# Attention's value products in three runs per pair of heads instead of four

## The chip, the cores and the metric

The kernel runs on one core of one Trainium2 chip. The metric is the device time of one execution in microseconds. Five engines work side by side, each through its own instructions in the order in which the program lists them: TensorE (PE, with its weight loads PEld), VectorE (DVE), ScalarE (ACT), GpSimd (POOL) and SyncE (SP), which issues the transfers. They meet at semaphores.

## The reference

```
q, k, v: (4 batches, 8 heads, 576 positions, 64)   all float32
scores = q k^T / 8 + bias(head, i, j)        # bias: a small two-layer net of log distances
attn   = softmax(scores)                     # row maximum taken off, divided by the row sum
x      = attn v                              # -> 2304 tokens x 512
x      = (h - tanh(h)) w_out,   h = x w_in                     # first layer, 512 -> 2048 -> 512
out    = (s relu(h)^2 + b) w2_out, h = x w2_in                 # second layer
```

## The kernel before, in words

**Stages.** The bias of every head is made first and goes to DRAM. Attention follows, then the two layers. All is float32, and the layers split each operand into a rounded upper part and a rest.

**Attention.** Work goes pair by pair: two heads of one batch, 16 pairs. A pair has five *periods*, one for each tile `t` of query rows: `t` = 0 to 3 are 128 rows of each head, `t` = 4 holds the last 64 rows of both heads in one tile. There are 80 periods, and the loop `for n in range(NK + 6)` takes each through a pipeline over the following turns. In turn `n` the program lists, in this order:

- `emit_norm(n - 2)`, POOL: the exponentials times the inverse row sum, into tile `pn`;
- `emit_score(n)`, PE: the scores into two PSUM tiles `s` (one for each head; there are two buffers);
- `emit_exp(n - 1)`, ACT: the exponentials with their row sums;
- `emit_bias(n)`, DVE: bias added to the scores, row minimum taken (`raw`, `mn`); this frees the tile `s`;
- `emit_transpose(n - 3)`, PE: `pn` is transposed 64 rows at a time into two PSUM banks `t0` and `t1` (and `c` for the tail columns of `t` = 0 and 1);
- `emit_parts(n - 3)`, the "bank copies": ACT copies `t0`, DVE copies `t1` into the tile `pt` of the unit. For `t` = 4 each makes three small copies. The banks have one buffer, so the next turn's transposes wait for both;
- `emit_sum(n - 1)` and `emit_inverse(n - 1)`, DVE: the inverse of the row sums;
- the value products of this turn (`emit_pv`, PE) from the table `PV`, and `emit_out` behind the last of a unit: ACT copies the result `o` to `xo`, SP stores it;
- the transfers of `FT` and `work`, then the weight steps of `TK`, then `PRE` (the first products of the first layer).

A pair has two *units* of value products: unit 0 (rows 0 to 255, `t` = 0 and 1) and unit 1 (rows 256 to 575). A unit is five key blocks `j`; each `j` is two products side by side, one for each head. The table gives unit 0 three blocks in turn 5i+6 and two in 5i+7, and unit 1 three in 5i+8 and two in 5i+10: four runs per pair, all at the end of their turn. As L436, L480 and L539 the profile shows scores, transposes and value products; their forms name the part of the array that they use (64\*128 for scores and transposes, 64\*64 for the scores of `t` = 4, 128\*64 for value products).

**Weight steps.** Eleven weight tiles of the layers are loaded during attention, and the first eight of them go through four steps there. `fetch(k)` loads tile `k` (turn 1 for `k` = 0). Step 0, `begin`, is one POOL and one ACT instruction on the loaded tile (L142, L143); steps 1 and 2, `high` and `low`, are one DVE instruction each (L148, L153); step 3, `both`, is a cast on ACT, a subtraction on POOL (L159, L98) and a store. `TK` says in which turn each is listed.

**After attention.** The first layer's first 512 tokens run in a plain loop; the rest of both layers goes in five groups `q`, each of eight steps `p`. In the groups 0 and 1 the function `keeps` lists the preparation of the second layer's weights at named places: `"S"` (start), `"A"` (middle) and `"E"` (end) of step `p`, and `"T"` (the tail of a group): load (`keep_raw`), `keep_begin`, `keep_value` (two DVE instructions and a store).

Of the kernel before, what the change touches and what calls it, by code (L numbers as in the profile page):

```python
# [19 lines left out]
B, H, S, D = 4, 8, 576, 64  # L20
# [27 lines left out]
FT = {1: 0, **{4 + 4 * k: k for k in range(1, 11)}}  # L48
ND = 8
TK = {}  # L50
for j, n in enumerate(sorted([41, *range(8, 80, 5)])):
    for m, step in ((n - n % 5, 0), (n, 1)) if j % 2 == 0 else ((n, 2), (n + 3, 3)):
        TK.setdefault(m, []).append((j // 2, step))
TK.update({82: [(8, 0)], 83: [(9, 0), (8, 1), (8, 2)], 84: [(10, 0), (9, 1), (9, 2)], 85: [(10, 1), (10, 2)]})
PR = [(0, 2), (2, 3)]
XPRE = [(-22, "load", 0), (-20, "hi", 0), (-19, "lo", 0), (-18, "load", 1), (-16, "hi", 1), (-15, "lo", 1),
        (-12, "load", 2), (-9, "hi", 2), (-8, "lo", 2), (-5, "load", 3), (-2, "hi", 3), (-1, "lo", 3)]


CHUNKS = [(0, 0, 512)]  # L60
# [6 lines left out]
def tile_kernel(ctx, tc, qk, vd, wcat, wts, sb, ltab, ipsi8, out):  # L67
# [39 lines left out]
    raw_w = {}  # L107
# [29 lines left out]
    def begin(k, raw):  # L137

        hw = raw[:, :, 1].bitcast(F32)
        x, sg = place(f"s{(0, 1, 6)[k % 3] if k < 32 else (0, 1, 6, 4, 5)[k % 5]}", [512]), place(f"s{2 + k % 2}", [512])  # L140
        y = ypool[0].tile([128, 512], F32, tag="y", name="y") if ypool else x
        nc.gpsimd.tensor_scalar(out=sg, in0=hw, scalar1=0.0, scalar2=1.0, op0=ALU.mult, op1=ALU.mult)  # L142
        nc.scalar.activation(out=y, in_=hw, func=AF.Copy, scale=2.0 ** -112)  # L143
        wx_t[k] = (raw, x, y, sg)
# [86 lines left out]
    with ExitStack() as c0:  # L231
# [63 lines left out]
        for n in range(NG + 2):  # L295
            if n < NG:
# [3 lines left out]
                for g in range(4 * G, 4 * G + 4):  # L300
                    hid = hids[g] = hp_.tile([128, LW], F32, tag="h", name="hid")
                    k = min(range(2), key=lambda k: held[k] + HC[k][0] + HC[k][1] * nd)
# [88 lines left out]
    with ExitStack() as ca:  # L391
# [15 lines left out]
        load, hi, lo = load_x(0)  # L407
# [30 lines left out]
        def emit_bias(x):  # L438
            i, t = periods[x]
            for j, k, _ in heads_of(x):  # L440
                raw = sp.tile([128, S], F32, tag="raw", name="raw", bufs=3)
                mn = sp.tile([128, 1], F32, tag="mn", name="mn", bufs=3)
                nc.vector.tensor_tensor_reduce(  # L443
                    out=raw.rearrange("p (c j) -> p c j", c=2), in0=s_t.pop((x, j))[:, :, 0:288],
                    in1=bias_t[pairs[i][0], k].rearrange("p (c j) -> p c j", c=2),
                    scale=-0.125, scalar=3.0e38, op0=ALU.add, op1=ALU.min, accum_out=mn)
                raw_t[x, j] = (raw, mn)

                if i >= 2 and bq and 36 - len(bq) < 11 + i // B * 9 + (max(0, k + 1) if i % B == B - 1 else 0):
                    load_bias(*bq.pop(0))  # L450

        def emit_exp(x):
            sm = sums[x] = sp.tile([128, 2], F32, tag="sm", name="sm", bufs=4)
            for j, _, _ in heads_of(x):
                raw, mn = raw_t.pop((x, j))
                p = p_t[x, j] = pp.tile([128, S], F32, tag="p", name="p")
                nc.scalar.activation(out=p, in_=raw, func=AF.Exp, scale=-1.0, bias=mn, accum_out=sm[:, j:j + 1])  # L457
# [72 lines left out]
        def emit_pv(i, u, j):  # L530

            r0, n = UNITS[u]
            v = v_t[i]
            if j == 0:
                o_t[i, u] = ps_o.tile([128, 512], F32, tag="o", name="o")[:, 0:n]
            o = o_t[i, u]
            for e in range(2):
                h = slice(e * 64, e * 64 + 64)
                nc.tensor.matmul(o[h], v[:, e, j], unit_t[i, u][:, 8 if j == 4 else 4 * e + j, 0:n], start=(j == 0), stop=(j == 4))  # L539

        def emit_out(i, u):
            hp, b = pairs[i]
            r0, n = UNITS[u]
            del unit_t[i, u]
            xo = sp.tile([128, 320], F32, tag="xo", name="xo", bufs=2)[:, 0:n]
            nc.scalar.copy(xo, o_t.pop((i, u)))
            nc.sync.dma_start(out=x1_d[hp][:, b * S + r0:b * S + r0 + n], in_=xo)
# [3 lines left out]

        PV = {}
        for i in range(len(pairs)):
            for u, (m, parts) in enumerate(((5 * i + 6, (3, 2)), (5 * i + 8, (3, 0, 2)))):
                js = list(range(5))
                for c, k in enumerate(parts):
                    PV.setdefault(m + c, []).append((i, u, js[:k]))
                    js = js[k:]
        for n in range(NK + 6):
            def now(lag):  # L560
                return 0 <= n - lag < NK

            if n == NK:
                s_ctx.close()
                for pool, name in ((hpool, "ps_h"), (ypool, "ps_y")):
                    pool.append(h_ctx.enter_context(tc.tile_pool(name=name, bufs=2, space=PSUM, side="right", reuse_waits="tile")))
            if now(2):
                emit_norm(n - 2)
            if now(0):
                emit_score(n)  # L570
            if now(1):
                emit_exp(n - 1)
            if now(0):
                emit_bias(n)
            if now(3):
                emit_transpose(n - 3)
                emit_parts(n - 3)
            if now(1):
                emit_sum(n - 1)
                emit_inverse(n - 1)  # L580
            for i, u, js in PV.pop(n, []):
                for j in js:
                    emit_pv(i, u, j)
                if 4 in js:
                    emit_out(i, u)
            if n in FT:
                fetch(FT[n])
            for f in work.pop(n, []):
                f()
            for k, j in TK.get(n, []):  # L590
                if j:
                    (high, low, both)[j - 1](k)
                else:
                    begin(k, raw_w.pop(k))
            for f in PRE.get(n, []):
                f()
        assert not PV
        assert not work
    qk_ctx.close()
# [2 lines left out]
    with ExitStack() as cb:  # L602
# [58 lines left out]
        def plan(at, g, j):  # L661
            KEEPS.setdefault(at, []).append((g, j))

        j = 0
        for P in range(1, 16):
            q, p = divmod(P, 8)
            three = P in (9, 11)
            for jj, at in ((j, "A"), (j + 1, "E")):
                plan((q, p, at), keep_value, jj)
                if P != 8:  # L670
                    plan((q, p - 1, "A" if P in (10, 12) else "S"), keep_raw, jj)
                    plan((q, p - 1, "E"), keep_begin, jj)
                else:
                    plan((0, 12, "T"), keep_raw, jj)
                    plan((0, 15, "T"), keep_begin, jj)
            if three:
                plan((q, p, "S"), keep_raw, j + 2)
                plan((q, p, "A"), keep_begin, j + 2)
                plan((q, p, "E"), keep_value, j + 2)
            j += 2 + three  # L680
# [3 lines left out]
        for n, f in enumerate(turns):  # L684
            if f not in ring_f.values():
# [5 lines left out]
                x = 16 - NR + n if n < 3 else max(ring_f, key=next_use)  # L691
# [188 lines left out]
        for _ in range(3):  # L880
            n, f, x, _ = back.pop(0)
# [209 lines left out]
```

## Time and profile before

| | |
|---|---|
| time, median of 3 runs | 1030.69 us (1029.17 to 1031.68) |
| the profiled execution's own time | 1030.39 us |
| its span, first to last instruction | 1028.6 us |
| PE busy | 1016.7 us (99%) |
| DVE, ACT, POOL busy | 719.7, 591.5, 571.5 us |
| attention's scores, first to last turn | 47.7 to 256.6 us |
| granted TensorE clock, in every slice | full speed |

The span is cut into times from its start. "Idle before" is the time that an engine stood still just before an instruction, and the name behind `<-` is what ended that. Matmuls are pipelined and their ends are modelled, so "busy" PE says only that no gap is seen; distances between starts say more.

### The profile page before, as it was taken

To read this page: it belongs to the slowest core of one execution; us is meant where nothing else is said; L and a number is where in the kernel's file an instruction comes from. 1 tells how busy PE (TensorE), PEld (TensorE's weight loads), DVE (VectorE), ACT (ScalarE), POOL (GpSimd) and SP (SyncE) were. 2 spreads that over 40 slices of the span, in tenths; PEclk is the share of its full clock that TensorE was granted. 3 is DMA by queue.
4 is the path that set the end of the run, shared out by engine and by line. 5 is a ranking of instruction groups with operands and counts; after the bars stand their busy time and mean duration, and the time that the engine had idled before them with its cause. 6 is when DMAs were issued, how large, how long until landed. Compare 5 with 4: busy or idle time off the path is not lost.

```text
span 1028.6 us, 18742 instructions
## 1 busy us (share of the span) xinstructions
PE 1016.7 (99%) x6664; PEld 830.9 (81%) x6664; DVE 719.7 (70%) x1478; ACT 591.5 (58%) x1241; POOL 571.5 (56%) x706
## 2 busy tenths in 40 slices
PE   9999999999999999999999999999999999999998
PEld 4366666666687799999788888999889998899986
DVE  8888888888478788876877776455675556655541
ACT  8888888888466555544544444455545444454441
POOL 3276676687468678840767431598516663076400
PEclk9999999999999999999999999999999999999999
DMA  8857575743399658867577648411202112031000
GB/s 293 316 190 252 182 254 170 229 152 103 113 360 340 250 206 280 285 210 250 196 268 235 205 143 291 154 41 42 100 14 93 45 58 92 3 104 49 1 32 31
DMA packets 68205, 170.48 MB, mean 166 GB/s; under 512 B 7312, under 2 KB 13584, under 8 KB 68112
## 3 DMA queue, kind: packets, MB, share of 16 engines
q1 hardware_dynamic: 67536, 168.80, 47.9%
q8 instruction: 52, 0.85, 0.3%
q10 hardware_dynamic: 576, 0.48, 0.1%
q14 instruction: 41, 0.34, 0.1%
HBM read 123.22 MB, written 46.04 MB: 165 GB/s over the span
## 4 chain that ended last, share of the span: by engine, by line
PE 86%; DVE 5%; POOL 1%; ACT 1%; DMA 1%; issue 1%; DVEq 0%; POOLq 0%; ACTq 0%
PE a L616 22%; PE o L539 8%; PE Z L923 8%; PE V L923 8%; PE s L436 7%; PE Y L923 6%; PE X L923 5%; PE V L616 5%; PE Z L616 5%; PE t L480 4%; PE h L371 2%; PE Y L616 2%; PE X L616 2%; DMA w<-x_d 1%; POOL C L98 1%
## 5 line engine op out<-in xcount | busy, mean ns | idle before, releaser
L98 POOL TENSOR_TENSOR C<-st,C 128x512 fp32r<-128x512 f32 x76 | 76.4, 1028 | 169.8 <-ACT C L741 130.7
L474 POOL TENSOR_SCALAR pn<-p,sm 128x576 f32<-128x576 f32 (+2 forms) x224 | 130.1, 597 | 52.5 <-DVE sm L465 21.5
L616 PE MATMUL a<-w,ring 128*128 128x512 f32 x576 | 146.6, 392 | 0.0
L616 PE MATMUL a<-ring,w 128*128 128x512 f32 (+1 forms) x576 | 127.5, 371 | 0.0
L616 PEld LDWEIGHTS a<-w,ring 128*128 128x128 f32 x576 | 107.5, 188 | 20.5
L443 DVE CUSTOM_DVE_ANT_0 raw<-s,bias 128x576 f32<-128x576 f32 x144 | 104.3, 753 | 21.7 <-PE s L436 18.6
L616 PEld LDWEIGHTS a<-ring,w 128*128 128x128 f32 x576 | 105.5, 188 | 14.9
L457 ACT ACTIVATE p<-raw,mn 128x576 f32<-128x576 f32 x144 | 110.7, 772 | 3.7 <-DVE mn L443 2.2
L98 POOL TENSOR_TENSOR C<-XB,C 128x512 fp32r<-128x512 f32 x80 | 106.9, 1359 | 0.0
L923 PE MATMUL Z<-C,C 128*128 128x384 f32 (+1 forms) x480 | 102.7, 347 | 1.9 <-DVE C L781 0.8
L436 PE MATMUL s<-qk 64*128 64x288 f32 (+1 forms) x640 | 92.5, 429 | 1.2 <-DVE mn L443 1.2
L923 PEld LDWEIGHTS Z<-C,C 128*128 128x128 f32 x480 | 85.3, 188 | 8.2 <-DVE C L781 2.1
L539 PE MATMUL o<-pt,vv 128*64 128x256 f32 (+1 forms) x640 | 91.5, 416 | 0.0
L142 POOL TENSOR_SCALAR s<-w 128x512 f32<-128x512 f32 x60 | 48.1, 803 | 54.1 <-DMA w<-in_wts 26.8
L436 PEld LDWEIGHTS s<-qk 64*128 64x128 f32 (+1 forms) x640 | 48.7, 175 | 35.5 <-DVE mn L443 19.9
L733 POOL TENSOR_TENSOR XB<-st 128x256 f32<-128x256 f32 x76 | 60.3, 793 | 18.0 <-DMA st<-win_d 15.8
L818 ACT ACTIVATE ring<-Y 128x384 f32<-128x384 f32 (+1 forms) x40 | 20.6, 514 | 74.0 <-PE Y L923 42.2
L818 ACT ACTIVATE ring<-X 128x384 f32<-128x384 f32 (+1 forms) x40 | 20.5, 514 | 71.7 <-DVE X L942 37.9
L480 PEld LDWEIGHTS t<-ident,pn 64*128 64x128 f32 x1248 | 52.1, 139 | 10.9 <-issue 2.9
L539 PEld LDWEIGHTS o<-pt,vv 128*64 128x64 f32 x640 | 40.3, 136 | 23.8 <-ACT ring L387 0.4
L480 PE MATMUL t<-ident,pn 64*128 64x64 f32 x1248 | 55.3, 223 | 0.8 <-POOL pn L474 0.8
L923 PE MATMUL V<-C,C 128*128 128x384 f32 (+1 forms) x240 | 50.9, 346 | 0.2 <-DVE C L781 0.2
(169 smaller groups left out, 2228.8 us busy)
## 6 DMA issues: line engine op xcount, KB each, us to landing
w<-in_wts SPq DMA_DIRECT2D x60, 512.0 KB, 5.0
w<-wsp_d SPq DMA_DIRECT2D x47, 512.0 KB, 5.5
st<-win_d SPq DMA_DIRECT2D x38, 512.0 KB, 3.8
qk<-in_qk SPq DMA_DIRECT2D x16, 864.0 KB, 5.3
bias_d<-m SPq DMA_DIRECT2D x36, 296.0 KB, 4.0
bias<-bias_d SPq DMA_DIRECT2D x32, 288.0 KB, 5.2
win_d<-s SPq DMA_DIRECT2D x32, 256.0 KB, 5.9
wsp_d<-w SPq DMA_DIRECT2D x16, 512.0 KB, 7.4
```

The costliest lines, as they stand in the source:

```text
L98: nc.gpsimd.tensor_tensor(out=lo, in0=raw, in1=hi.bitcast(F32), op=ALU.subtract)
L142: nc.gpsimd.tensor_scalar(out=sg, in0=hw, scalar1=0.0, scalar2=1.0, op0=ALU.mult, op1=ALU.mult)
L436: nc.tensor.matmul(o[0:n, c, 0:288], q[h, ee, t * 128:t * 128 + n], kk[h, ee], start=True, stop=True)
L443: nc.vector.tensor_tensor_reduce(out=raw.rearrange("p (c j) -> p c j", c=2), in0=s_t.pop((x, j))[:, :, 0:288], in1=bias_t[pairs[i][0], k]. ...
L457: nc.scalar.activation(out=p, in_=raw, func=AF.Exp, scale=-1.0, bias=mn, accum_out=sm[:, j:j + 1])
L474: nc.gpsimd.tensor_scalar(out=pn[:, c:c + b - a], in0=p[:, a:b], scalar1=sm[:, j:j + 1], scalar2=0.0, op0=ALU.mult, op1=ALU.add)
L480: nc.tensor.transpose(out_, in_, ident[ROWS[r], ROWS[r]])
L539: nc.tensor.matmul(o[h], v[:, e, j], unit_t[i, u][:, 8 if j == 4 else 4 * e + j, 0:n], start=(j == 0), stop=(j == 4))
L616: nc.tensor.matmul(o, x, y, start=first and j == 0, stop=last and j == 2)
L733: nc.gpsimd.tensor_tensor(out=o, in0=a, in1=b, op=op)
L818: nc.scalar.activation(out=t, in_=c, func=(AF.Tanh, AF.Relu)[layer])
L923: nc.tensor.matmul(o, cs[:, a, l, i * 128:i * 128 + 128], unit(q, u, i, r), start=begins and i == 0 and j == 0, stop=i == 1 and j == 2, sk ...
```

## The change

- **Value products.** Unit 0's five blocks come as one run in turn 5i+7, listed between that turn's scores and its transposes. Unit 1 keeps its two runs.
- **Exponentials.** In turns with `n % 5 == 2` the exponentials of turn `n` itself are listed too, ahead of the run of five; in turns with `n % 5 == 3` none are listed.
- **Result copies.** `emit_out` is listed behind the exponentials and ahead of the bank copies: for unit 0 in the same turn, for unit 1 in the next one.
- **Weight steps.** `high` and `low` come in turns `n % 5 == 2`, ahead of the bank copies (before: `n % 5 == 3`, at the end); `begin` in turns `n % 5 == 3` (before: 0), so that tile 0 is begun in turn 3 instead of 5; `both` in turns `n % 5 == 3` (before: 1). The one irregular place moves from turn 41 to 43.
- **Token split.** The rest of the last token tile (`lo` of 3) goes from turn 79 to turn 80.
- **Keeps.** The two weights that were loaded and begun in the tail of group 0 and finished in step 0 of group 1 are spread over group 1: its steps 5 and 7 take three weights now, as 1 and 3 did.

```diff
-for j, n in enumerate(sorted([41, *range(8, 80, 5)])):
-    for m, step in ((n - n % 5, 0), (n, 1)) if j % 2 == 0 else ((n, 2), (n + 3, 3)):
+for j, n in enumerate(sorted([43, *range(7, 80, 5)])):
+    for m, step in ((n - 4, 0), (n, 1)) if j % 2 == 0 else ((n, 2), (min(81, n + 6 - n % 5 // 3), 3)):
...
-        (-12, "load", 2), (-9, "hi", 2), (-8, "lo", 2), (-5, "load", 3), (-2, "hi", 3), (-1, "lo", 3)]
+        (-12, "load", 2), (-9, "hi", 2), (-8, "lo", 2), (-5, "load", 3), (-2, "hi", 3), (0, "lo", 3)]
...
-            for u, (m, parts) in enumerate(((5 * i + 6, (3, 2)), (5 * i + 8, (3, 0, 2)))):
+            for u, (m, parts) in enumerate(((5 * i + 7, (5,)), (5 * i + 8, (3, 0, 2)))):
...
+        def values(n):
+            for i, u, js in PV.pop(n, []):
+                for j in js:
+                    emit_pv(i, u, j)
+                if 4 in js:
+                    outs.append((i, u))
+        def steps(n, which):
+            for k, j in [x for x in TK.get(n, []) if x[1] in which]:
+                TK[n].remove((k, j))
+                if j:
+                    (high, low, both)[j - 1](k)
+                else:
+                    begin(k, raw_w.pop(k))
...
             if now(0):
                 emit_score(n)
-            if now(1):
+            if now(1) and n % 5 != 3:
                 emit_exp(n - 1)
+            while outs:
+                emit_out(*outs.pop())
             if now(0):
                 emit_bias(n)
+            if n % 5 == 2:
+                if now(0):
+                    emit_exp(n)
+                values(n)
+                while outs:
+                    emit_out(*outs.pop())
+                steps(n, (1, 2))
             if now(3):
                 emit_transpose(n - 3)
                 emit_parts(n - 3)
...
-        for P in range(1, 16):
+        for P in (*range(1, 8), *range(9, 16)):
             q, p = divmod(P, 8)
-            three = P in (9, 11)
+            three = P in (9, 11, 13, 15)
...
-                if P != 8:
-                    plan((q, p - 1, "A" if P in (10, 12) else "S"), keep_raw, jj)
-                    plan((q, p - 1, "E"), keep_begin, jj)
-                else:
-                    plan((0, 12, "T"), keep_raw, jj)
-                    plan((0, 15, "T"), keep_begin, jj)
+                plan((q, p - 1, "A" if P in (10, 12, 14) else "S"), keep_raw, jj)
+                plan((q, p - 1, "E"), keep_begin, jj)
```

## Rows read from the trace of the kernel before

**Rows 1.** Windows, one pair: us, then busy us of each engine (instructions), clock, DMA.
```profile
162.20:175.65 13.45, 13.45 (x164) 8.86 (x162) 11.63 (x37) 11.10 (x30) 9.43 (x16) 1.00 0.56 178
```

**Rows 2.** Waits of PE over the whole span: us in total, times, longest us.
```profile
PE s L436 <- DVE mn L443: 1.2, 4, 0.5
PE t L480 <- POOL pn L474: 0.8, 1, 0.8
```

**Rows 3.** Timeline, PE alone, turns 45 to 48: start us, length us, instructions merged.
```profile
163.54 1.19 PE L436 MATMUL s<-qk 64*128 64x288 f32 x7
164.52 0.71 PE L480 MATMUL t<-ident,pn 64*128 64x64 f32 x16
...
166.52 1.24 PE L436 MATMUL s<-qk 64*128 64x288 f32 x8
167.59 0.66 PE L480 MATMUL t<-ident,pn 64*128 64x64 f32 x16
168.18 1.51 PE L539 MATMUL o<-pt,vv 128*64 128x256 f32 x12
169.63 1.24 PE L436 MATMUL s<-qk 64*128 64x288 f32 x8
170.70 0.60 PE L480 MATMUL t<-ident,pn 64*128 64x64 f32 x14
171.23 1.08 PE L539 MATMUL o<-pt,vv 128*64 128x256 f32 x8
172.24 1.24 PE L436 MATMUL s<-qk 64*128 64x288 f32 x8
```

**Rows 4.** Timeline of turns 46 and 47: bias on DVE, bank copies of `t` = 4.
```profile
167.32 0.76 DVE L443 CUSTOM_DVE_ANT_0 raw<-s,bias 128x576 f32<-128x576 f32 x1 [0.38 <-PE s L436]
...
168.68 0.08 DVE L443 DVE_READ_ACCUMULATOR2_ANT mn<- 128x1 f32 x1
...
171.33 0.37 ACT L524 COPY pt<-t 128x256 f32<-128x256 f32 x1 [0.75 <-PE t L480]
...
171.79 0.42 DVE L524 COPY pt<-t 128x256 f32<-128x256 f32 x1
...
172.46 0.29 DVE L526 COPY pt<-t 128x128 f32<-128x128 f32 x1
```

**Rows 5.** Transfer and timeline at attention's start (the second row: KB, us to landing).
```profile
53.64 0.58 SPq L115 DMA_DIRECT2D w<-in_wts  x1
...
w<-in_wts SPq DMA_DIRECT2D x1, 512.0 KB, 4.0
...
55.31 0.78 ACT L457 ACTIVATE p<-raw,mn 128x576 f32<-128x576 f32 x1
...
56.84 0.57 ACT L522 COPY pt<-t 128x512 f32<-128x512 f32 x1
...
57.62 0.72 PE L480 MATMUL t<-ident,pn 64*128 64x64 f32 x16
...
59.07 0.69 ACT L143 ACTIVATE s<-w 128x512 f32<-128x512 f32 x1
```

**Rows 6.** Timeline at attention's end: a cast on ACT and its operand.
```profile
256.58 0.67 DVE L153 SCALAR_TENSOR_TENSOR s<-w,s 128x512 int32<-128x512 int32 x1
...
264.58 0.59 ACT L522 COPY pt<-t 128x512 f32<-128x512 f32 x1 [3.15 <-PE t L480]
...
265.07 0.62 ACT L159 CAST w<-s 128x512 fp32r<-128x512 f32 x1
```

**Rows 7.** Timeline, turns 59 to 62: POOL ahead of the transposes of `t` = 2.
```profile
202.46 1.97 POOL L474 TENSOR_SCALAR pn<-p,sm 128x576 f32<-128x576 f32 x3 [0.63 <-ACT p L457]
...
204.87 0.71 PE L480 MATMUL t<-ident,pn 64*128 64x64 f32 x16
...
210.84 1.27 POOL L98 TENSOR_TENSOR C<-s,C 128x512 fp32r<-128x512 f32 x1
```

**Rows 8.** Timeline in the first steps of group 1.
```profile
498.46 1.67 PE L923 MATMUL Z<-C,C 128*128 128x512 f32 x6 [0.30 <-DVE ring L837]
```

More of the change, by code (lines that the diff above doesn't have):

```diff
@@ L558, in tile_kernel @@
                     js = js[k:]
+        outs = []
+        def values(n):
[11 more added lines that the diff above has]
+                    begin(k, raw_w.pop(k))
         for n in range(NK + 6):
@@ L580, in tile_kernel @@
                 emit_inverse(n - 1)
[L581 to L585, printed above, removed]
+            values(n)
             if n in FT:
@@ L589, in tile_kernel @@
                 f()
-            for k, j in TK.get(n, []):
-                if j:
-                    (high, low, both)[j - 1](k)
-                else:
-                    begin(k, raw_w.pop(k))
+            steps(n, range(4))
             for f in PRE.get(n, []):
                 f()
+        while outs:
+            emit_out(*outs.pop())
         assert not PV
@@ L664, in tile_kernel @@
         j = 0
-        for P in range(1, 16):
+        for P in (*range(1, 8), *range(9, 16)):
             q, p = divmod(P, 8)
-            three = P in (9, 11)
+            three = P in (9, 11, 13, 15)
             for jj, at in ((j, "A"), (j + 1, "E")):
                 plan((q, p, at), keep_value, jj)
-                if P != 8:
-                    plan((q, p - 1, "A" if P in (10, 12) else "S"), keep_raw, jj)
-                    plan((q, p - 1, "E"), keep_begin, jj)
-                else:
-                    plan((0, 12, "T"), keep_raw, jj)
-                    plan((0, 15, "T"), keep_begin, jj)
+                plan((q, p - 1, "A" if P in (10, 12, 14) else "S"), keep_raw, jj)
+                plan((q, p - 1, "E"), keep_begin, jj)
             if three:
```

## The prediction

> **What bounds the kernel now.** I read the windows of one pair first: in 13.45 us TensorE shows 13.45 us busy, VectorE 11.63, ScalarE 11.10 and GpSimd 9.43 [rows 1]. So in attention TensorE is the bound and the other three have 14 to 30% to spare, on average. Then the waits of TensorE: all of its waits on attention's helpers are about 2 us in the whole span, 1.2 for the bias on VectorE and 0.8 for `pn` from GpSimd [rows 2]; these fall at attention's start and end. So within a pair the order before hides every helper completely. What TensorE loses it loses between its own blocks; the PE timeline shows it [rows 3]. The reader is to see there that a run of value products has a fixed price: 12 instructions take 168.18 to 169.63 = 1.45 us, 8 take 171.23 to 172.24 = 1.01, which is 0.11 each and 0.13 besides. Transposes show the same at their end: 16 take 0.59 to the next run, 14 take 0.53, so 0.03 each and 0.11 besides.
>
> **The run that goes.** Turns 46 to 48 before: scores 1.07, transposes 0.59, run of three 1.45, scores 1.07, transposes 0.53, run of two 1.01; sum 5.72 = 172.24 - 166.52 [rows 3]. After: scores 1.07; transposes 0.48 (no run behind them); scores straight behind transposes 1.02 (163.54 to 164.52 for 7 of 8 instructions, and the block before ends some 0.05 earlier); then scores to run, which the trace does not show: taken as transposes to run, 0.11 (the nearest row), bounds 0 and 0.25; run of five 20 x 0.11 + 0.13 = 2.33; run to transposes, also not shown, is in the 0.13, bounds -0.1 to 0.2 more; transposes 0.42. Sum 5.43, so 0.29 less, and the next scores, behind transposes instead of a run, 0.05 less again. As the two changes that aren't shown are likelier to cost more than less, I take 0.27 us saved per pair, bounds 0.0 and 0.45. That is TensorE's own time, if nothing makes it wait.
>
> A rule of the Trainium skill bears on this ("TensorEngine Tiling (Array Packing)", Key Properties): changing the tiling mode, and not just the tile, drains the engine. Transposes to values change from 64\*128 to 128\*64 and show the 0.11, so the trace agrees. By that rule two drains per pair go, and nothing else changes: it is the first rival below. The same page says nothing of what the drains were hiding, and that is where the trace speaks against the change.
>
> **What the run was hiding.** Three waits appear, each from rows.
>
> *Scores wait for the bias.* Two score tiles have two buffers. The bias of a turn starts 167.32 - 166.52 = 0.80 us behind its scores and ends for both tiles at 168.68 + 0.08 = 168.76, 2.24 behind [rows 3, 4]. Before, the next scores came 3.11 us behind. After, in turns 1 of a pair nothing but transposes lies between: the next scores come 1.07 + 0.48 = 1.55 behind, their second tile half a block (0.5) later, 2.05 to 2.1, against 2.24 and the signal. I take 0.18 us of wait, bounds 0.05 and 0.4.
>
> *Transposes wait for the bank copies of `t` = 4.* VectorE's three copies take 171.79 to 172.46 + 0.29 = 0.96 us, and a copy starts about 0.25 us behind the start of the last transpose (170.70 + 0.60 - 0.22, to 171.33) [rows 3, 4]: the banks are free 1.2 to 1.25 us behind it. Before, a run of 1.01 and scores of 1.07 covered that. After, only scores do, 1.05. I take 0.19, bounds 0 and 0.5. ScalarE's copies now stand behind two exponentials and the result copy of the same turn; counted through (bias ends, two exponentials of 0.77, copy 0.27, bank copies 0.6) they end about when VectorE's do, so an exponential that slips adds to this wait: that is its upper bound.
>
> *Transposes of `t` = 2 wait for GpSimd.* Before, `pn` ends at 202.46 + 1.97 = 204.43 and its transposes start at 204.87: 0.44 us in reserve [rows 7]. After, the inverse row sums come about as much later, since VectorE takes the bias of a turn behind the late copies of `t` = 4; the reserve is gone. In the seven turns into which `both` moves, its GpSimd subtraction of 1.27 us [rows 7] now stands directly ahead of this `pn`: I take 0.13 each and 0.7 in turn 48, which has a `begin` too, 1.6 us together; bounds 0 and 7 x (1.27 - 0.44) = 5.8.
>
> Per pair -0.27 + 0.18 + 0.19 = +0.10, times 14 pairs behind the start = +1.4; with the 1.6 the steady part is +3.0 (bounds -3.8 = no waits, and about +8).
>
> **The start.** `begin(0)` goes from turn 5 to turn 3, the load stays where it is. It is issued at 53.64 and lands 4.0 us later, at 57.64 [rows 5]; SP reaches it only behind the bias loads, which the change doesn't touch. Before, `begin(0)` ran on ScalarE at 59.07, behind the landing. In turn 3 it stands ahead of the exponentials of turn 3, which started at 55.31. ScalarE goes in order: at the end of attention its cast, with an operand made at 256.58, waited until 265.07 behind a bank copy for which ScalarE idled 3.15 us [rows 6]. So: 57.64, the `begin` some 0.6, two exponentials and the gap to the copy 1.53 (55.31 to 56.84), bank copy 0.57: 60.35, and the transposes of turn 5 wait for it; before they ran at 57.62 [rows 5]. Cost 2.8 us, bounds 2.0 and 3.5. Queued behind it are VectorE's row sums and with them the next bias, and on GpSimd, whose half of `begin` waits for the same landing, `pn` of the next turn; both are late by as much or less, so they add nothing. Nothing gives it back: from 62 us on TensorE was the bound.
>
> **The end and the layers.** The 0.8 us that transposes waited for `pn` [rows 2] fell on turn 80; there the exponentials of turn 77 now run a turn earlier. I take -0.7, bounds -1.0 and +0.3 (the moved `lo` stands ahead of the first layer's product in the same turn, but is needed only in its last instructions). In group 1 two value steps, four VectorE instructions, leave step 0, where TensorE waits at 498.46 for the last of that chain [rows 8]; the gap and the slow restarts around it are 0.85 together: -0.7, bounds -0.85 and 0. The added weights in steps 5 and 7 lie where TensorE has no gap and VectorE a quarter of its time free: 0, at worst their VectorE time in one step, +1.5. The SP queue holds the same transfers in nearly the same order: 0.
>
> **Sum.** 2.8 + 3.0 - 0.7 - 0.7 = +4.4 on the profiled execution's own 1030.39 (span 1028.6 and 1.8 around it) = 1034.8; that execution lies 0.3 under the median of the runs shown, so I say 1035.0.
>
> **Rivals.**
> - *The waits are covered (not slower).* If bias and copies are ready when asked, the whole 0.27 counts: -3.8 in the steady part, 2.8 at the start, -1.4 behind: -2.4, 1028.2. It decides at one point: a second bias done under 2.05 us behind its scores and copies of `t` = 4 under 1.05 behind their transposes. Against it, 2.24 and 1.2 above; for it, that both are close.
> - *The load is there in time.* Then the start costs nothing: 1032.0 with the waits, 1025.4 without. For it only that SP's bias loads might go faster; nothing moves them.
> - *The helpers become the bound.* If `pn` and the exponentials run late in every pair and not in seven turns, 0.3 more per pair: +4.2, 1039.2. For it, VectorE at 86% before with its work now bunched in turns 2 and 3.
> - *The order isn't what the list says* and nothing changes: 1030.7. ScalarE's order in the trace follows the list, so hardly.
>
> **How the numbers follow.** Forecast (1032.5 to 1037) 0.54; waits covered 0.21; load in time 0.07 with waits and 0.03 without; helpers the bound 0.13; nothing 0.02. A measurement of this kernel can tell about 0.3%, 3.1 us, from no change: 1027.6 to 1033.8. Slower: most of the forecast (0.45) and 0.13 = 0.58. Faster: 0.03 and a third of the covered case's lower half, 0.04 = 0.07. Within: 0.35. The range reaches down through part of the covered case and up to the helpers' case: 1029.0 to 1039.0; the likeliest case's own range is 1032.5 to 1037.
>
> **What would show it.** In the changed kernel's timeline: ScalarE's first `begin` near 57.7 with the transposes of turn 5 behind 60; a pair of 13.5 to 13.7 us by the starts of its score blocks; waits of `s` for `mn` and of `t` for the copies of L524 to L526, once per pair each; no gap near 498. The prediction is wrong if a pair takes under 13.3 us, if those waits are missing, or if the first transposes are where they were.

## The result and the profile after

The changed kernel takes 1041.15 us (median of 5 runs, 1040.91 to 1042.07), the kernel before 1030.32 beside it: a ratio of 1.0105, 95% interval 1.0093 to 1.0116, so 10.8 us slower. The forecast was 1035.0, with a range of 1029.0 to 1039.0. The direction was right, the size was not. The profiled execution's own time is 1041.15, its span 1039.4.

Cut at the starts of TensorE's score blocks of `t` = 4, which come once per pair, the 10.8 us of span come from these places:

| stretch | before, us | after, us | difference |
|---|---|---|---|
| up to the first scores | 47.70 | 47.09 | -0.6 |
| first pair behind the start | 13.36 | 16.18 | +2.8 |
| the next 14 pairs | 188.5 | 197.2 | +8.7 |
| from the last scores of `t` = 4 to the first product of the five groups | 95.9 | 95.6 | -0.3 |
| the five groups of the layers | 676.1 | 676.3 | +0.2 |

The 7.03 us between the first scores and the first block of `t` = 4 are the same in both. Up to the first scores nothing was changed; there the traces of all runs lie between 46.9 and 47.7 us.

Of the 14 pairs, 12 take 14.04 us where they took 13.45, and two take 14.36 and 14.39. By turns, 3, 4, 0, 1, 2 of a period: 3.43, 1.32, 2.97, 3.11, 2.62 before; 3.96, 1.32, 2.97, 1.62, 4.16 after. Turns 1 and 2 together, from which a run of value products went, are 5.78 in place of 5.72, and turn 3, in which nothing was added for TensorE, is 0.53 longer.

One pair of the changed kernel by windows, with the columns of [rows 1]; TensorE is no longer busy throughout, and VectorE has 0.7 us more:

```profile
164.62:178.67 14.05, 13.78 (x169) 8.74 (x166) 12.31 (x37) 10.79 (x29) 8.56 (x14) 1.00 0.45 150
```

Waits of TensorE over the span of the changed kernel, as in [rows 2], and one of ScalarE from the list for all engines:

```profile
PE t L480 <- issue: 4.4, 15, 0.6
PE t L480 <- ACT pt L522: 3.1, 2, 2.3
...
PE s L436 <- DVE mn L443: 1.2, 4, 0.5
```

```profile
ACT p L457 <- POOL pn L474: 11.6, 30, 0.6
```

The waits of `t` are new: 2.3 us of the second row is the start, and the first row comes once per pair. It is put down to "issue", that is to nothing the profile names; the timeline shows what it was. ScalarE's row is the first hint: 30 exponentials waited for GpSimd.

Timeline of the changed kernel, turns 1 to 3 of one pair (start, length, engine); TensorE's rows answer to [rows 3], the copies to [rows 4]:

```profile
172.88 1.24 PE L436 MATMUL s<-qk 64*128 64x288 f32 x8
...
173.96 0.66 PE L480 MATMUL t<-ident,pn 64*128 64x64 f32 x16
...
174.37 0.08 DVE L443 DVE_READ_ACCUMULATOR2_ANT mn<- 128x1 f32 x1
...
174.51 1.43 PE L436 MATMUL s<-qk 64*128 64x288 f32 x8
...
175.05 0.08 DVE L443 DVE_READ_ACCUMULATOR2_ANT mn<- 128x1 f32 x1
...
175.87 2.38 PE L539 MATMUL o<-pt,vv 128*64 128x256 f32 x20
...
176.20 2.14 POOL L474 TENSOR_SCALAR pn<-p,sm 128x576 f32<-128x576 f32 x3 [1.66 <-DVE sm L465]
...
177.27 0.89 DVE L153 SCALAR_TENSOR_TENSOR s<-w,s 128x512 int32<-128x512 int32 x1
...
178.18 0.65 PE L480 MATMUL t<-ident,pn 64*128 64x64 f32 x14
178.38 0.78 ACT L457 ACTIVATE p<-raw,mn 128x576 f32<-128x576 f32 x1 [0.52 <-POOL pn L474]
...
178.67 1.19 PE L436 MATMUL s<-qk 64*128 64x288 f32 x8
178.90 0.42 DVE L524 COPY pt<-t 128x256 f32<-128x256 f32 x1 [0.74 <-PE t L480]
...
179.15 0.35 ACT L546 COPY xo<-o 128x256 f32<-128x256 f32 x1
...
179.40 0.37 ACT L524 COPY pt<-t 128x256 f32<-128x256 f32 x1
179.58 0.29 DVE L526 COPY pt<-t 128x128 f32<-128x128 f32 x1
...
179.77 0.26 ACT L526 COPY pt<-t 128x128 f32<-128x128 f32 x1
...
180.13 0.81 PE L480 MATMUL t<-ident,pn 64*128 64x64 f32 x16 [0.27 <-issue]
```

Read it from the end. Transposes of turn 3 start 180.13 - 178.67 = 1.46 us behind their scores; unhindered it is 1.07 in the kernel before, behind a run, and 1.03 in e4_exp3 below, behind transposes as here. VectorE's three copies out of its bank end at 179.87, ScalarE's at 180.03, and TensorE starts 0.1 behind the latter. ScalarE's are late because the exponential ahead of them started at 178.38 only, at the moment GpSimd's three `pn` operations (176.20 + 2.14) had ended. There are four `p` buffers; in the new order an exponential of turn 2 takes the one that GpSimd is still reading. And `pn` takes 2.14 there where it takes 1.70 in other turns, beside VectorE's integer step, which takes 0.89 where it took 0.67 [rows 6].

Higher up, scores of turn 2 take 1.43 us in place of 1.24. Single instructions of the trace show why: the first head starts 0.05 us late (112 ns behind the last transpose, where it is 60 in turn 3) and the second 0.09 late, both 0.06 behind the end of the bias of the tile that they need (174.45 and 175.13), and behind each late start the next instruction comes later too, 340 ns on in place of 295 (first head, as in turn 3) and of 236 (second). So 0.14 us of waiting became 0.29. The step from scores to the run of five, unseen before, is 332 ns in place of 236, 0.10.

The start, as in [rows 5]:

```profile
52.65 0.58 SPq L115 DMA_DIRECT2D w<-in_wts  x1
...
56.65 0.67 ACT L143 ACTIVATE s<-w 128x512 f32<-128x512 f32 x1 [1.84 <-DMA w<-in_wts]
...
57.22 0.76 ACT L457 ACTIVATE p<-raw,mn 128x576 f32<-128x576 f32 x1
...
58.74 0.56 ACT L522 COPY pt<-t 128x512 f32<-128x512 f32 x1
...
59.44 0.71 PE L480 MATMUL t<-ident,pn 64*128 64x64 f32 x16 [2.33 <-ACT pt L522]
```

The load lands 4.0 us behind its issue, `begin` waits 1.84 for it ahead of two exponentials and the copy, and the transposes wait 2.33, as the prediction had it. They come 12.36 us behind the first scores; before, it was 9.92.

At attention's end TensorE's wait in turn 80 is as long as it was, now put down to ScalarE's bank copy. Before:

```profile
258.12 0.58 ACT L522 COPY pt<-t 128x512 f32<-128x512 f32 x1 [0.94 <-PE t L480]
...
258.84 0.76 PE L480 MATMUL t<-ident,pn 64*128 64x64 f32 x16 [0.77 <-POOL pn L474]
```

After:

```profile
269.06 0.58 ACT L522 COPY pt<-t 128x512 f32<-128x512 f32 x1 [1.10 <-PE t L480]
...
269.79 0.76 PE L480 MATMUL t<-ident,pn 64*128 64x64 f32 x16 [0.77 <-ACT pt L522]
```

In the layers the gap of [rows 8] is gone, and another of about 0.6 us has come at the other end of group 1, where four value steps on VectorE now stand (0.33 idle, and slow restarts around it):

```profile
612.34 1.82 DVE L148 SCALAR_TENSOR_TENSOR s<-s,s 128x512 int32<-128x512 int32 x1
...
617.06 0.73 PE L636 MATMUL X<-ring,w 128*128 128x512 f32 x2 [0.33 <-DVE ring L853]
```

### The profile page after: what moved, and what is told of

The parts are those of the page before. It is cut to its first block, busy times and chain, and to the rows that moved or that the text cites. A ratio compares the mean times of both kernels' runs of the same rounds, so it can differ in the third digit from the quotient of the medians.

```text
span 1039.4 us, 18733 instructions
## 1 busy us (share of the span) xinstructions
PE 1020.9 (98%) x6664; PEld 829.5 (80%) x6664; DVE 725.9 (70%) x1478; ACT 593.2 (57%) x1241; POOL 574.1 (55%) x706
## 4 chain that ended last, share of the span: by engine, by line
PE 85%; DVE 4%; issue 3%; DMA 3%; POOL 2%; ACT 2%; SPq 0%; POOLq 0%; DVEq 0%; ACTq 0%
PE a L636 21%; PE o L539 8%; PE Z L939 8%; PE V L939 8%; PE s L436 7%; PE Y L939 6%; PE X L939 6%; PE Z L636 5%; PE V L636 5%; PE t L480 4%; PE h L371 2%; PE X L636 2%; PE Y L636 2%; POOL m L284 1%; DMA w<-x_d 1%
## 5 line engine op out<-in xcount | busy, mean ns | idle before, releaser
L474 POOL TENSOR_SCALAR pn<-p,sm 128x576 f32<-128x576 f32 (+2 forms) x224 | 132.5, 608 | 70.0 <-DVE sm L465 60.1
L436 PE MATMUL s<-qk 64*128 64x288 f32 (+1 forms) x640 | 94.6, 431 | 1.2 <-DVE mn L443 1.2
L539 PE MATMUL o<-pt,vv 128*64 128x256 f32 (+1 forms) x640 | 88.0, 413 | 0.0
L480 PE MATMUL t<-ident,pn 64*128 64x64 f32 x1248 | 58.6, 226 | 7.6 <-issue 4.4
L522 ACT COPY pt<-t 128x512 f32<-128x512 f32 x64 | 37.4, 584 | 33.1 <-PE t L480 30.4
```

The lines of the kernel that those rows point to most:

```text
L436: nc.tensor.matmul(o[0:n, c, 0:288], q[h, ee, t * 128:t * 128 + n], kk[h, ee], start=True, stop=True)
L474: nc.gpsimd.tensor_scalar(out=pn[:, c:c + b - a], in0=p[:, a:b], scalar1=sm[:, j:j + 1], scalar2=0.0, op0=ALU.mult, op1=ALU.add)
L480: nc.tensor.transpose(out_, in_, ident[ROWS[r], ROWS[r]])
```

## The experiments

Turn numbers are by the period's place, as above. "Pairs" is the time from one score block of `t` = 4 to the next. Ratios are to the kernel before, run beside each (medians 1029.5 to 1030.4). A *position* P of the layers' prepared weights is step P - 8 of group 1 for P from 8 to 15.

**Four versions of the changed kernel: start, buffers, weight step, exponentials.**

```diff
  e1_begin5
-    for m, step in ((n - 4, 0), (n, 1)) if j % 2 == 0 else ...
+    for m, step in ((max(5, n - 4), 0), (n, 1)) if j % 2 == 0 else ...
  e2_sixp
-        pp = ... name="pp", bufs=4    np_ = ... name="np_", bufs=5
+        pp = ... name="pp", bufs=6    np_ = ... name="np_", bufs=4
  e3_hl3: TK lists high and low for turn 3, and in turn 2
-                steps(n, (1, 2))
  e4_exp3
-            if now(1) and n % 5 != 3:
+            if now(1):
...
             if n % 5 == 2:
-                if now(0):
-                    emit_exp(n)
```

e1_begin5: 

> The changed kernel with one edit undone: weight tile 0 is begun in turn 5 again, not in turn 3. Theory (ScalarE in order waits for the landing): the first transposes of turn 5 come back from 12.35 us behind the first scores to about 9.9, the pairs stay at 14.04 us, the time falls by 2.3 to 2.8 to about 1038.5. Rival (the start was late for another reason, or the loss is only moved): the transposes of turn 5 stay beyond 12 us, time 1041.

Measured: 1040.54 us (1038.88 to 1046.19), ratio 1.0122 [1.0093, 1.0152], too scattered to tell. The trace tells: the first pair takes 14.28 in place of 16.18, the others are as in the changed kernel, and the transposes of turn 5 come 9.86 us behind the first scores in place of 12.36:

```profile
57.03 0.72 PE L480 MATMUL t<-ident,pn 64*128 64x64 f32 x16
```

So 1.9 us of the first pair's 2.82 are the load's. Of the other 0.9, 0.6 are the waits that every pair has; 0.3 lie in the pair's turn 1, which takes 0.58 us longer than in later pairs (before, 0.26).

e2_sixp: 

> The changed kernel with six buffers for the exponentials instead of four (and four for the normalized tile instead of five, to make room). Theory A (the second exponential of turn 2 waits for GpSimd to free a buffer, and so ScalarE's bank copies and the next transposes are late): the waits of exponentials for GpSimd go, the transposes of turn 3 start when VectorE's copies end, 0.2 us earlier, a pair takes about 13.85 us, time about 1038.5. Rival B (ScalarE simply has too much listed ahead of its bank copies, buffers or not): pair 14.04, time 1041.

Measured: 1038.72, ratio 1.0088 [1.0073, 1.0103]; pairs 13.80, and 14.01 where the weight's last step falls.

e3_hl3: 

> The changed kernel with the VectorE weight steps (high, low) at the end of turn 3 again instead of in turn 2. Theory A: GpSimd's normalizing in turn 2 takes 1.70 us again instead of 2.14, since VectorE's integer step no longer runs beside it, the second exponential and ScalarE's bank copies come 0.4 us earlier, and a pair takes about 13.85 us (VectorE's copies end last then); time about 1038.5. Rival B: ScalarE's list is unchanged, so the pair stays at 14.04. Rival D (the steps now delay the bias of turn 4 or the normalizing of turn 2's rows): a new wait of transposes for pn, pair 14.1 or more.

Measured: 1044.87, ratio 1.0144 [1.0128, 1.0159]. Turn 3 takes 3.73 us in place of 3.96, so moving the integer step away from GpSimd's `pn` helps turn 3 as much as more buffers do. Most pairs without that last step take 13.81 to 13.95, a few 14.05 to 14.29; most others take 14.53, one 14.92, because the transposes of `t` = 2 now wait for `pn`. The whole is slower.

e4_exp3: 

> The changed kernel with the exponentials of a turn n % 5 == 2 listed in the next turn, as before the change, and nothing else moved. Theories A and B both: ScalarE's bank copies of t = 4 follow the transposes at once, VectorE's copies end last, pair about 13.85 us, time about 1038.5. Rival C (VectorE's three copies alone make the wait of the next transposes): no change, 14.04. Should the pair fall under 13.7, the wait for VectorE's copies that is left was smaller than 0.2 us.

Measured: 1038.20, ratio 1.0080 [1.0065, 1.0095]; pairs 13.80, one 14.33. Three different edits take the same 0.24 us off turn 3, and each leaves turn 2 at 4.16. So the chain is shown: integer step, `pn`, `p` buffer, exponential, ScalarE's copies, transposes. What is left in e4_exp3 is VectorE's bank:

```profile
164.10 1.19 PE L436 MATMUL s<-qk 64*128 64x288 f32 x8
164.30 0.37 ACT L524 COPY pt<-t 128x256 f32<-128x256 f32 x1 [0.20 <-PE t L480]
164.34 0.42 DVE L524 COPY pt<-t 128x256 f32<-128x256 f32 x1 [0.74 <-PE t L480]
...
165.01 0.29 DVE L526 COPY pt<-t 128x128 f32<-128x128 f32 x1
165.13 1.01 PE L480 MATMUL t<-ident,pn 64*128 64x64 f32 x16
```

The first transpose, into ScalarE's bank, starts in time, 1.03 behind the scores; VectorE's bank is free at 165.30, the second transpose starts at 165.45 with the other 14 behind it, and the block takes 1.01 in place of 0.66. Turn 3 is 3.72 against 3.43: 0.29 us. This part is read from the timeline; the edit that was to free VectorE's bank sooner, g3_copies below, did not do so, but in f1_five_end2, where a run covers the copies again and the helpers keep their old order, turn 3 is back at 3.43.

**Four versions of the kernel before, each with one part of the change.**

```diff
  f1_five_end2 (f2_five_end1: 5 * i + 6)
-            for u, (m, parts) in enumerate(((5 * i + 6, (3, 2)), ...
+            for u, (m, parts) in enumerate(((5 * i + 7, (5,)), ...
  f3_keeps: of the changed kernel the last hunk alone
  f4_steps: of the changed kernel TK and XPRE alone
```

f1_five_end2: 

> The kernel before with one line changed: unit 0's five blocks as one run in turn 5i+7, listed at the end of the turn as all runs were; weight steps, exponentials, copies and keeps as before. Theory (each run saves 0.27 us and what it covered is lost): the run still covers the bank copies of t = 4, so that wait does not appear; in turn 1 of a pair scores follow scores with transposes alone between, and wait 0.2 us for the bias. Pair 13.45 - 0.27 + 0.22 = 13.40 us, time within 0.3% of before (1029.0). Rival (the placement between scores and transposes is not what costs): a pair near 13.8 as in the changed kernel with the exponentials put back.

Measured: 1034.82, ratio 1.0049 [1.0037, 1.0062]; pairs 13.51, every other one 13.95. Missed. Turn 3 is back at 3.43: with the run of five between the transposes of turn 2 and the scores of turn 3, the bank copies have time. But turn 2 takes 4.17, so the scores' wait eats the saving.

f2_five_end1: 

> The kernel before with unit 0's five blocks as one run in turn 5i+6, at the end of the turn. Theory: the wait of scores for the bias in turn 1 does not appear; in turn 2 the transposes of t = 4 are followed by scores alone, so the next transposes wait 0.3 us for VectorE's copies. Pair 13.45 - 0.27 + 0.30 = 13.48 us, time the same (1030). Rival (waits come from somewhere else, such as GpSimd): pair beyond 13.6; or (the saving of a run is larger than its covers) under 13.35.

Measured: 1040.52, ratio 1.0105 [1.0091, 1.0119]; pairs 13.92 and 14.25, turn 3 4.02 and 4.36. Missed: with the run one turn earlier turn 2 is the short one (1.62), and both the scores (1.43 long, as above) and the transposes of turn 3 come too early.

f3_keeps: 

> The kernel before with only the changed list of keeps (second layer's weights in group 1). Theory from the two traces: the gaps near the start of group 1 (0.85 us together) go and gaps of about 0.6 come at its tail, where three weights stand in step 7; attention untouched at 13.45 us per pair; time the same as before within 0.5 us. Rival (the prediction's): 0.7 us shorter.

Measured: 1029.03, ratio 0.9995 [0.9986, 1.0004], pairs 13.45. The gap at 498 goes, one of about 0.6 us comes at 604.8.

f4_steps: 

> The kernel before with only the weight steps of attention in the changed turns (begin in turns 3, high and low in turns 2, both in turns 3, token split one turn later), value products and exponentials as before. Theory: the start loses 2 to 2.8 us to the landing of tile 0. In the pairs with both in turn 3 GpSimd's 1.27 us stand ahead of the normalizing of t = 2, which had 0.44 us in reserve: at most 0.8 us each in seven pairs, most likely 0.2 to 0.5; in all other pairs 13.45. Time about 1034 to 1036. Rival (the steps are hidden in the order before): pairs all 13.45, time 1032.

Measured: 1034.99, ratio 1.0053 [1.0039, 1.0067]. The first pair takes 15.30 (+1.94); pairs with the weight's last step 13.73, others 13.45.

**Where the third weight stands; three runs elsewhere; the bank copies.**

```diff
  g1_keeps14: before, with position 8 free
-            three = P in (9, 11)
+            three = P in (9, 11, 13, 14)
...
  g2_runs123: before
-    ((5 * i + 6, (3, 2)), (5 * i + 8, (3, 0, 2)))
+    ((5 * i + 7, (5,)), (5 * i + 8, (3, 0, 0, 2) if i < 15 else (3, 0, 2)))
  g3_copies: e4_exp3, the third copy of t = 4 (g4_all: with e1_begin5's line too)
-                    copy(pt[:, 8, 0:256]...[:, :, r], ab[r][:, 5:7])
+                    nc.scalar.copy(pt[:, 8, 0:256]...[:, :, r], ab[r][:, 5:7])
```

g1_keeps14: 

> The kernel before with its attention untouched; of the layers' prepared weights, position 8 is left free as in the changed kernel, and the positions with three weights are 9, 11, 13 and 14 in place of 9, 11, 13 and 15. Theory (the gap at 498 goes wherever position 8 is free; the new gap of about 0.6 us near 605 to 617 comes from the third weight at position 15): pairs of 13.45 us as before, no gap at 498 and none at group 1's end, 0.7 to 1.5 us under the kernel before, about 1028.8. Rival (the value steps of VectorE at that place are late whichever position takes the third weight): a gap of 0.5 us or more somewhere between 560 and 620 us, time within 0.3 us of the kernel before.

Measured: 1028.76, ratio 0.9986 [0.9977, 0.9995], no gap at 498 and none at the other end of the group. Held: the third weight at position 15 is what made the new gap.

g2_runs123: 

> The kernel before, weight steps and all, with three runs of value products per pair, in turns 2 (five), 3 (three) and 1 of the next period (two), each at its turn's end as before; nothing else is moved. Theory (what three runs lose is the waits of the run of five that stands right before scores): the wait of turn 3's scores for the bias and the weight steps' turn take more than the run saves, pairs of 13.5 us or more, time 1032 to 1036. Rival (three runs save 0.27 us per pair wherever no transposes stand behind the run of five): pairs of 13.2 to 13.3 us, time 1026 to 1028.

Measured: 1034.62, ratio 1.0045 [1.0032, 1.0057], pairs 13.73 (some 13.78 to 14.4). The size held, the place did not. TensorE's timeline, turns 1, 2 and 3:

```profile
153.68 1.43 PE L436 MATMUL s<-qk 64*128 64x288 f32 x8 [0.16 <-DVE mn L443]
154.95 0.73 PE L480 MATMUL t<-ident,pn 64*128 64x64 f32 x16
155.61 1.30 PE L539 MATMUL o<-pt,vv 128*64 128x320 f32 x8
156.84 1.24 PE L436 MATMUL s<-qk 64*128 64x288 f32 x8
157.91 0.60 PE L480 MATMUL t<-ident,pn 64*128 64x64 f32 x14
158.44 2.38 PE L539 MATMUL o<-pt,vv 128*64 128x256 f32 x20
160.75 1.24 PE L436 MATMUL s<-qk 64*128 64x288 f32 x8
```

Here turn 0 has no run, and the scores of turn 1 wait (1.43). Those of turn 2, behind a run, do not, and turn 2 with the run of five takes 3.91, where f1_five_end2 took 4.17: 0.26 us are the wait of the second turn's scores with what it takes along. It is the scores behind a turn without a run that wait, wherever that turn is.

g3_copies: 

> The changed kernel with turn 2's exponentials left in turn 3 (which measured 1038.2 us and pairs of 13.80) and with ScalarE, not VectorE, making the third copy of the bank of the last tile in one half (VectorE's pair of copies in turn 3 falls from two to one, 0.29 us earlier; ScalarE has one more). Theory (VectorE's copies set the start of turn 3's transposes there): transposes start 0.2 to 0.3 us sooner, turn 3 is 3.45 to 3.55 us, pairs 13.5 to 13.6, time 1034 to 1035. Rival (ScalarE's copies end as late as VectorE's once it has one more): pairs stay at 13.75 to 13.9, time 1037.5 to 1038.5.

Measured: 1040.81, ratio 1.0099 [1.0083, 1.0114], pairs 13.79 and 14.11. Missed. The copy went to ScalarE, and the bank came free no sooner:

```profile
165.20 1.19 PE L436 MATMUL s<-qk 64*128 64x288 f32 x8
...
165.87 0.23 DVE L525 COPY pt<-t 64x64 f32<-64x64 f32 x1
...
166.19 0.27 ACT L526 COPY pt<-t 128x128 f32<-128x128 f32 x1 [0.15 <-DVE pt L525]
...
166.51 0.57 PEld L480 LDWEIGHTS t<-ident,pn 64*128 64x128 f32 x15 [0.27 <-ACT pt L526]
```

ScalarE's second copy waits for VectorE's and ends at 166.46, 1.26 behind the scores; in e4_exp3 VectorE's ended 1.20 behind. The three copies of one bank are one chain, whichever engines make them. This agrees with the Trainium skill ("PSUM — Partial Sum Buffer", "PSUM bank collisions raise a hardware error"), by which two engines must not touch the same part of a bank at once and are kept apart by dependencies. Every other pair loses 0.32 besides, in transposes that wait for `pn`.

g4_all: 

> The kernel of the run before this one, and the beginning of the first weight in turn 5 in place of turn 3. Theory (start, exponentials' chain and bank copies are the three places where the change loses): first pair within 0.9 us of the others, pairs 13.5 to 13.6, time 1031 to 1033, so with all three repaired the three runs still don't beat the kernel before. Rival (the run's saving of 0.27 us per pair comes through once the waits are gone): pairs 13.2 to 13.3, time 1026 to 1028.

Measured: 1037.98, ratio 1.0079 [1.0067, 1.0092]. The first pair is 14.03 against 17.07 in g3_copies: the start's wait is gone, 3.0 us. The pairs are those of g3_copies, so the time expected for both theories was missed.

**What the other 0.35 us per pair is.** At that point 0.24 of 0.59 us was shown.

```diff
  h1_begin3: f1_five_end2, begin of a weight in turn 3
-    ((n - n % 5, 0), (n, 1)) if j % 2 == 0
+    ((max(5, n - 5), 0), (n, 1)) if j % 2 == 0
  h2_tails: h1_begin3 (h3_keeps: with g1_keeps14's positions too)
-            if t == 2:
-                emit_tails(1, x - 2)
+            if t == 3:
+                emit_tails(1, x - 3)
...
  h4_changed_tails: the same tails, in e4_exp3 with e1_begin5's line
```

h1_begin3: 

> The kernel before with the run of five at the end of turn 2 (which measured pairs of 13.51 and, in every other pair, 13.95) and each weight's beginning two turns earlier, in turn 3 in place of turn 0 (the first stays in turn 5). Theory (the 0.44 us of every other pair is ScalarE's half of the beginning, 0.69 us ahead of turn 0's exponentials, so that the bias waits for a free buffer): all pairs 13.51, time 1031.5 to 1032.5. Rival (it is the cast at the end of turn 1, which stays): every other pair stays at 13.9 to 14.0, time 1034.8.

Measured: 1031.86, ratio 1.0017 [1.0008, 1.0026], all pairs 13.52. Held. In f1_five_end2 this is a pair of the slower kind:

```profile
155.22 0.69 ACT L143 ACTIVATE s<-w 128x512 f32<-128x512 f32 x1
...
156.69 0.76 DVE L443 CUSTOM_DVE_ANT_0 raw<-s,bias 128x576 f32<-128x576 f32 x1 [0.34 <-ACT p L457]
...
157.51 0.76 PE L436 MATMUL s<-qk 64*128 64x288 f32 x4 [0.35 <-DVE mn L443]
```

The beginning of a weight holds up an exponential, this the bias, for want of a `raw` buffer, and this the scores. In the kernel before a run of three stood there and hid it.

h2_tails: 

> The run before this one, and the two tail transposes of t = 0 and 1 (with the copy behind them on ScalarE) one turn later, behind the transposes of turn 1, so that 0.22 us of TensorE's work moves from turn 0, which has a run, to turn 1, which has none. Theory (scores of turn 2 come 1.55 to 1.62 us behind those of turn 1 and wait for a chain scores, bias, scores that is about 0.3 us longer whatever VectorE's load): the wait nearly goes, turn 1 about 1.77, turn 2 about 3.9, pairs 13.2 to 13.3, time 1028 to 1029. Rival (VectorE or ScalarE is behind in turn 1 by its load, and the later copy of 0.38 us adds to it): turn 2 stays at 4.15 or grows, pairs 13.5 or more, time 1032 or more.

Measured: 1029.90, ratio 0.9993 [0.9984, 1.0002]; pairs 13.39. Turn 0 falls by 0.12. Counted from the first instruction of each score block, turns 1 and 2 stay at 1.62 and 4.17, with 0.12 us more work in turn 1. TensorE, turns 1 to 3 (the row at 154.22 lacks the first instruction of its block, which starts at 154.14):

```profile
152.52 1.24 PE L436 MATMUL s<-qk 64*128 64x288 f32 x8
...
154.22 1.36 PE L436 MATMUL s<-qk 64*128 64x288 f32 x7
155.41 0.66 PE L480 MATMUL t<-ident,pn 64*128 64x64 f32 x14
156.00 2.38 PE L539 MATMUL o<-pt,vv 128*64 128x256 f32 x20
158.31 1.24 PE L436 MATMUL s<-qk 64*128 64x288 f32 x8
```

So the wait is a chain of fixed length that work can cover, as the theory says, and not a load. The expected 13.2 to 13.3 was too much: the tails weigh 0.12, not 0.22, so 0.12 of the 0.29 of waiting is covered and the rest is still lost.

h3_keeps: 

> The run before this one with the prepared weights of the layers as in g1_keeps14, which gave 1028.8 us against 1030.0 alone. Theory: 1.2 us under the run before this one, about 1027, below both kernels by 3 us or more. Rival (the attention part doesn't gain): 1030 or more.

Measured: 1028.69, ratio 0.9984 [0.9975, 0.9993]. It and g1_keeps14 are the best versions, each 1.2 to 1.7 us below the kernel before, and they can't be told apart. The pairs' 0.06 x 14 = 0.8 us is mostly given back in the first pair, 13.75 against 13.36, and behind the last: from the last scores of `t` = 4 to the end of the value products it takes 17.32 against 16.74. So a gain from the three runs themselves isn't shown in the whole time.

h4_changed_tails: 

> The changed kernel with turn 2's exponentials left in turn 3 and the first weight's beginning in turn 5 (each measured alone: pairs of 13.80; 2 us at the start), and the two tail transposes in turn 1 as in the second run here. Theory (of the 0.35 us that pairs of 13.80 lie over 13.45, the scores' wait in turn 2 is about 0.3 and goes, the transposes' wait in turn 3 is about 0.29 and stays, the saving is 0.27): turns 1 and 2 together 5.45 to 5.55 us plus the 0.22 moved, turn 3 about 3.72, pairs 13.5 to 13.6, time 1032 to 1034. Rival (the waits in turn 2 are not the bias's chain): pairs 13.75 or more, time 1036 or more.

Measured: 1033.74, ratio 1.0030 [1.0019, 1.0042]; pairs 13.68, one 14.22. Turns 1 and 2 stay at 5.79, turn 3 at 3.72. The tails' 0.12 is won here too; the time lies in the range expected, the pairs 0.1 above it. Moving the other two tail transposes as well, which might cover the rest, was not tried: both pairs write one bank, and would have to be kept apart by a wait.

## Why the prediction was wrong

- **The run that goes, 0.27 us per pair: right.** Scores to run was taken as 0.11 and is 0.10. Turns 1 and 2 after, 5.78, less the 0.29 of the next point, are 5.49 against 5.72: 0.23. By another way, turn 2 with the run of five and without a wait takes 3.91 (g2_runs123); with the 1.55 of turn 1 that the prediction worked out, 5.46: 0.26. No run showed both turns without any wait.
- **Scores wait for the bias, 0.18: place right, size 0.29.** The delay of the two heads' starts, 0.05 and 0.09, is what the prediction counted (0.05 to 0.1 for the second tile, and the signal). It left out that each late start slows the instruction behind it, another 0.15. It lies within its bounds (0.05 to 0.4), but it alone turns the saving into nothing: turns 1 and 2 came out at 5.78 against 5.72.
- **Transposes wait for the bank copies of `t` = 4, 0.19 with an upper bound of 0.5: the step that failed, 0.53.** VectorE's copies, from which the 0.19 was worked out, come as late as it said but cost 0.29 (e4_exp3): the transpose that waits starts 0.15 behind the end of the last copy (165.30 to 165.45), and the count had nothing for that. The other 0.24 is ScalarE's copies. The prediction counted their chain through and said they "end about when VectorE's do"; they ended 0.16 later, since the exponentials ahead of them waited for GpSimd to free a `p` buffer. The count had the durations of two exponentials, and not the four buffers. The prediction named the place ("an exponential that slips adds to this wait"), and gave it no price of its own, only the upper bound.
- Of the 6.1 us between forecast and result this one term is 0.34 x 14 = 4.8, and the scores' wait 0.11 x 14 = 1.5. Per pair, -0.23 + 0.29 + 0.53 is the 0.59 that the pairs of 14.04 have over 13.45.
- **Transposes of `t` = 2 wait for GpSimd, 1.6: too high.** It shows in one pair, 0.32, behind the turn 48 for which the prediction took 0.7, and not in seven. The 0.35 of the other long pair belongs to the term above: in its turn 3 the exponential behind `pn` starts 0.34 later against the scores than in the other pairs, and the bank copies' wait is 0.62 us in place of 0.27. In f4_steps it is 0.28 in each pair with a last step, in e3_hl3 0.7, in e2_sixp 0.2 and in g3_copies 0.32; in the changed kernel most such pairs don't show it. I take it that the other waits give GpSimd the time there; that is argued, not shown.
- **The start, +2.8: place and mechanism right**, and the first pair is 2.82 longer. By e1_begin5 1.9 of it is the load, a little under the bounds (2.0 to 3.5); f4_steps has 1.94 for it, g4_all against g3_copies 3.0. Of the rest 0.6 is the waits of a pair, which the prediction counted for 14 pairs and not for the first. SP issued the load 1.0 us earlier, 0.6 of it because the first scores came earlier, so the transposes started at 59.44 and not at 60.35; from the first scores they are 2.44 later.
- **The end, -0.7: mechanism wrong, most of the size by chance.** The wait of 0.8 us that was to go is still there. Before, too, the copy ended only 0.14 ahead of these transposes (258.70 to 258.84), so an earlier `pn` had little to win. What was won is 0.22 in the last of the 14 pairs, which was longer than the others and is not now, and 0.3 behind it; of that, 0.26 is a wait in the first layer for VectorE, 0.80 before and 0.54 after, which f3_keeps doesn't have and h3_keeps has with 1.01.
- **The layers, -0.7: wrong, +0.2.** The gap at 498 goes as said. "The added weights lie where TensorE has no gap: 0" failed: f3_keeps shows a new gap for the old one (-0.89 and +0.62 us), g1_keeps14 that position 15 made it. The changed kernel's groups lose another 0.57 in their first 16 us, at waits for VectorE (0.2 us each at 374.86 and 375.86). f4_steps has this too, e2_sixp and f3_keeps haven't; its cause is open.
- **Rivals.** "The helpers become the bound" was nearest: one of its two, the exponentials, is late in every pair and costs 0.24 (it said 0.3). "The waits are covered" fell at the point it named: VectorE's bank is free at 179.87, 1.26 us behind the start of the last transpose (178.18 + 0.65 - 0.22), where it asked for 1.05, and the second bias ends 2.25 behind its scores (172.88 to 175.13), where it asked for 2.05.

## What to carry to other kernels

A block of work that hides latencies has a value that its own time doesn't show: before merging two such blocks, count for each helper chain (producer, helper, the producer's next use of the buffer) how far the next use now lies behind, and look for the chain that has no other block to cover it. Count buffers as well as durations: an operation moved ahead needs a free output buffer at its new time, and who frees it is often an engine that the edit doesn't touch. Here merging paid about 0.25 us and opened waits of 0.82 per pair; the merge began to pay, by 0.06 a pair, only when the run stood at the end of its turn, a small piece of other work was moved into the turn left without a run, and one helper's operation was moved to another turn. Even then the whole time didn't show it (h2_tails, ratio 0.9993).

## What the runs showed of the hardware

- A matmul stream that waits 0.05 to 0.09 us loses about as much again behind the wait: the next instruction comes after 340 ns in place of 236 to 295, so that 0.14 us of waiting cost 0.29. The same 340 ns stand behind the first scores after a run, where nothing waits.
- Beside VectorE's integer step GpSimd's `pn` group took 2.14 us in place of 1.70: by single instructions 0.75, 0.69 and 0.75, the last one over 64 columns, which takes 0.32 alone; the integer step took 0.89 in place of 0.67. Both lost, by 0.4 and 0.2. In the kernel before, the integer step starts first (202.18) and keeps its 0.67, and GpSimd alone loses: its group takes 1.97 [rows 7]. This agrees with the Trainium skill ("SBUF — State Buffer", "SBUF: two separate sides"): a VectorE operation with two inputs in SBUF and a GpSimd operation that reads SBUF exclude each other for a whole instruction.
- When the two banks of a transpose block come free at different times, the later one holds up the block: in e4_exp3 one transpose went at 165.13 and the other 15 from 165.45 on, and the block took 1.01 us against 0.66. From the end of the last copy to the transpose that waits for it were 0.15 us there, and 0.10 in the changed kernel (180.03 to 180.13).
